# A long convolution's second stage on four frequencies at once, one in each quarter of the TensorE array

## The chip, the cores and the metric

One core of one Trainium2 chip. The time is that of the device for the whole kernel, in microseconds (us), over several runs; smaller is better.

## The reference

A long convolution by FFT along the sequence for 8 batches, then a soft mixture of experts. Cut to what matters:

```python
# x: (8, 5696, 128), h: (5696, 128), all float32
Xf = np.fft.rfft(x, n=2 * S, axis=1); Hf = np.fft.rfft(h, n=2 * S, axis=0)
x = np.fft.irfft(Xf * Hf[None], n=2 * S, axis=1)[:, :S, :].reshape(B * S, D)
logits = x @ phi                       # phi: (128, 32)
# dispatch: softmax of the logits over the tokens; experts on 32 slots;
# combine: softmax over the slots, out = c @ slot_out
```

## The kernel before

The transform is split into 90 x 64. **Stage one** (`stage_a`) multiplies blocks of x by a table of 90 frequencies and stores the result. **Stage two** (`stage_b1`, `stage_b2`) works on 45 pairs of frequencies per batch, two pairs in a *unit*, 23 units per batch: forward transform of length 64, product with the filter's transform (`Hr`, `Hi`), backward transform. **Stage three** (`stage_c1` to `stage_c6`) transforms back, computes the logits and both softmaxes. A loop of 92 steps interleaves them; one batch takes 8 steps. Stage one runs in steps 0 to 71, stage two from step 9, stage three from step 26. A step has three slots for stage-two units.

Cut to what the change and the argument touch (`...` marks cuts):

```python
ps = mid.enter_context(tc.tile_pool(name="ps", bufs=6, space=PSUM))    # bank(): a ring of 6 banks
aps = mid.enter_context(tc.tile_pool(name="aps", bufs=2, space=PSUM))
wt = fconst.tile([P, NP, P], F32, name="wt")    # P = 128, NP = 45: block-diagonal 2 x (64 x 64)
vt = fconst.tile([P, NP, P], F32, name="vt")
...
    def stage_b1(u):
        g, i = divmod(u, NU)
        n = min(2, NP - 2 * i)
        t_ = gs.pop(u)
        p = bank()
        pv = p[:, :].rearrange("p (q c d) -> p q c d", c=2, d=D)
        for q in range(n):
            nc.tensor.matmul(p[:, q * 256:(q + 1) * 256], wt[:, 2 * i + q, :],
                             t_[:, q, :, :].rearrange("p c d -> p (c d)"), start=True, stop=True)
        if g == 0:
            for q in range(n):
                m = 2 * i + q
                pr = bpool.tile([P, 2, D], F32, name="pr", tag="pr")
                for c in range(2):
                    nc.scalar.activation(pr[:, c, :], pv[:, q, c, :], AF.Copy,
                                         scale=turn[:, 0, m:m + 1])
                nc.vector.scalar_tensor_tensor(
                    out=Hr[:, m, :], in0=pv[:, q, 1, :], scalar=turn[:, 1, m:m + 1],
                    in1=pr[:, 0, :], op0=AL.mult, op1=AL.add)
                nc.vector.scalar_tensor_tensor(
                    out=Hi[:, m, :], in0=pv[:, q, 0, :], scalar=turn[:, 1, m:m + 1],
                    in1=pr[:, 1, :], op0=AL.mult, op1=AL.subtract, reverse1=True)
            return
        pr, pi = [bpool.tile([P, 2, 2, D], F32, name=f"p{c}", tag=f"p{c}") for c in "ri"]
        for t, H in ((pr, Hr), (pi, Hi)):
            nc.vector.tensor_tensor(
                out=t[:, 0:n, :, :], in0=pv[:, 0:n, :, :],
                in1=H[:, 2 * i:2 * i + n, :].unsqueeze(2).broadcast_to([P, n, 2, D]), op=AL.mult)
        y_ = bpool.tile([P, 2, 2, D], F32, name="yf", tag="yf")
        nc.vector.tensor_tensor(out=y_[:, 0:n, 0, :], in0=pr[:, 0:n, 0, :], in1=pi[:, 0:n, 1, :],
                                op=AL.subtract)
        nc.vector.tensor_tensor(out=y_[:, 0:n, 1, :], in0=pr[:, 0:n, 1, :], in1=pi[:, 0:n, 0, :],
                                op=AL.add)
        prods[u] = y_

    def stage_b2(u):
        g, i = divmod(u, NU)
        if g == 0:
            return
        n = min(2, NP - 2 * i)
        y_ = prods.pop(u)
        p = bank()
        for q in range(n):
            nc.tensor.matmul(p[:, q * 256:(q + 1) * 256], vt[:, 2 * i + q, :],
                             y_[:, q, :, :].rearrange("p c d -> p (c d)"), start=True, stop=True)
        st = bpool.tile([P, 2, 2 * D], F32, name="zst", tag="zst", bufs=3)
        nc.scalar.activation(st[:, 0:n, :], p[:, 0:n * 256].rearrange("p (q c) -> p q c", q=n),
                             AF.Copy)
        nc.sync.dma_start(
            out=zd[g - 1][2 * i:2 * i + n, :, :, :].rearrange("q r c d -> r q (c d)"),
            in_=st[:, 0:n, :])
...
    def stage_c3(T):
        ...                                       # TensorE: logits; ScalarE: lt
            nc.vector.reduce_max(out=mx[r, :], in_=lt[r, :, :, 0:MH - v], axis=AX.XYZ)   # mx
        ...
        def slot_b():
            if us:
                u = us.pop(0)
                prefetch(u + AHEAD)
                stage_b1(u)
                wait_b2.append(u)
                if len(wait_b2) > 1:
                    stage_b2(wait_b2.pop(0))
            elif wait_b2:
                stage_b2(wait_b2.pop(0))
        ...
        if t < NA:
            stage_a(t, 1)
            fold(t + 1, 1)                        # GpSimd: x of the next block
        if pair(1) is not None:
            stage_c3(pair(1))
        slot_b()
```

In the traces TensorE's matmuls and VectorE's instructions stand in the order in which they are issued here. So the backward half of a unit comes one slot after its forward half.

Of the kernel before, what the change touches and what calls it, by code (L numbers as in the profile page):

```python
# [17 lines left out]
def transform_tables(S, N1, N2, CH, Z0, X0, F0):  # L18
# [18 lines left out]
    s1 = np.pad(s1, [(X0, P - R1 - X0), (0, 0), (F0, P - N1 - F0)])  # L37
# [7 lines left out]
    NP = N1 // 2  # L45
    back = np.arange(N2).reshape(2, HALF // CH, CH).transpose(1, 0, 2).reshape(-1)
    wbd = np.zeros((2 * N2, NP, 2 * N2))
    vbd = np.zeros((2 * N2, NP, 2 * N2))
    for par in range(2):
        r = slice(par * N2, (par + 1) * N2)  # L50
        wbd[par::2, :, r] = w[par * NP:(par + 1) * NP].transpose(1, 0, 2)
        vbd[r, :, r] = w[par * NP:(par + 1) * NP][:, back].transpose(2, 0, 1)
    turn = (N1 - 1) / 2 * alpha[:, None] + (N2 - 1) / 2 * omega
    tn = np.zeros((2 * N2, 2, NP))
    for par in range(2):
        r = slice(par * N2, (par + 1) * N2)
        tn[r, 0] = np.cos(turn[par * NP:(par + 1) * NP]).T / N
        tn[r, 1] = np.sin(turn[par * NP:(par + 1) * NP]).T / N
    return [np.ascontiguousarray(t, dtype=np.float32) for t in (s1, i1, wbd, vbd, tn)]
# [3 lines left out]
def kernel(  # L63
# [24 lines left out]
    nc = tc.nc  # L88
# [18 lines left out]
    Z0, X0, F0 = 20, 20, 19  # L107
# [4 lines left out]
        for n, t in zip(("s1", "i1", "w", "v", "turn"), transform_tables(S, N1, N2, CH, Z0, X0, F0))]  # L112
    fd = [nc.dram_tensor(f"f_{g}", (N2, N1, 2, D), F32, kind="Internal").ap() for g in range(B + 1)]
# [16 lines left out]
    ypool = work.enter_context(tc.tile_pool(name="ypool", bufs=1))  # L130
    mid, inner, cload = ExitStack(), ExitStack(), ExitStack()
    ps = mid.enter_context(tc.tile_pool(name="ps", bufs=6, space=PSUM))
    aps = mid.enter_context(tc.tile_pool(name="aps", bufs=2, space=PSUM))
    front = ExitStack()
# [6 lines left out]
    wt = fconst.tile([P, NP, P], F32, name="wt")  # L141
    vt = fconst.tile([P, NP, P], F32, name="vt")
    turn = fconst.tile([P, 2, NP], F32, name="turn")
    Hr = fconst.tile([P, NP, D], F32, name="Hr")
    Hi = fconst.tile([P, NP, D], F32, name="Hi")

    def bank():
        return ps.tile([P, 512], F32, name="bank", tag="bank")
# [34 lines left out]
    def stage_a(c, comp):  # L183
# [4 lines left out]
        for G in range(2):  # L188
# [6 lines left out]
        nc.sync.dma_start(out=fd[g][n0:n0 + CH, :, :, :].rearrange("n k g d -> k n (g d)"),  # L195
                          in_=st[F0:F0 + N1, :, :, :].rearrange("k n g d -> k n (g d)"))
# [4 lines left out]
    def load_g(u):  # L201
        if u >= (B + 1) * NU:
# [6 lines left out]
            in_=fd[g].rearrange("r (a p) c d -> (r a) (p c d)",  # L209
                                a=2)[:, 4 * i * D:(4 * i + 2 * n) * D])  # L210
        gs[u] = t_

    def stage_b1(u):
# [3 lines left out]
        p = bank()  # L217
        pv = p[:, :].rearrange("p (q c d) -> p q c d", c=2, d=D)
        for q in range(n):
            nc.tensor.matmul(p[:, q * 256:(q + 1) * 256], wt[:, 2 * i + q, :],  # L220
                             t_[:, q, :, :].rearrange("p c d -> p (c d)"), start=True, stop=True)
        if g == 0:
            for q in range(n):
                m = 2 * i + q
                pr = bpool.tile([P, 2, D], F32, name="pr", tag="pr")
                for c in range(2):
                    nc.scalar.activation(pr[:, c, :], pv[:, q, c, :], AF.Copy,  # L227
                                         scale=turn[:, 0, m:m + 1])
                nc.vector.scalar_tensor_tensor(  # L229
                    out=Hr[:, m, :], in0=pv[:, q, 1, :], scalar=turn[:, 1, m:m + 1],  # L230
# [6 lines left out]
        for t, H in ((pr, Hr), (pi, Hi)):  # L237
            nc.vector.tensor_tensor(  # L238
                out=t[:, 0:n, :, :], in0=pv[:, 0:n, :, :],
                in1=H[:, 2 * i:2 * i + n, :].unsqueeze(2).broadcast_to([P, n, 2, D]), op=AL.mult)  # L240
# [522 lines left out]
```

## Time and profile before

| | before |
|---|---|
| median of all its runs | 1062.6 us |
| span of the profiled run | 1066.3 us |
| steps 0 to 9 | 60.1 us |
| steps 10 to 16 (h in stage two) | 50.7 us |
| steps 17 to 25 (stages one and two) | 85.6 us |
| steps 26 to 70 (all three stages) | 591.3 us |
| from step 71 | 278.6 us |
| one cycle of 8 steps in the middle stage | 104.8 us |

In the stretch of steps 10 to 16, the busy times of the engines (columns: stretch, length, then busy us of TensorE, its weight loads, VectorE, ScalarE, GpSimd, each with a count; the clock; the DMA share; GB/s) were:

```profile
60.10:110.80 50.70, 42.95 (x136) 24.63 (x135) 23.63 (x80) 35.98 (x107) 17.16 (x14) 1.00 0.93 279
```

DMA is at 0.93 there, so it looks as if the kernel were held by its transfers while h passes stage two. The waits of ScalarE in this stretch say otherwise (who waited for whom: us in total, times, longest):

```profile
ACT pr L227 <- DVE Hi L232: 14.7, 20, 0.7
```

It is ScalarE's only wait there. Its 36.0 us of work and these 14.7 us fill the 50.7 us: ScalarE and VectorE, which hand `pr` and its buffers to each other, set the pace (e1 below has less DMA and the same length). In the middle cycle (the third stretch that the prediction below shows) TensorE is the bound. Two lines of the waits in that cycle (who waited for whom: us in total, times, longest):

```profile
DVE mx L358 <- ACT lt L352: 8.4, 4, 2.2
PEld bank L256 <- DVE yf L244: 1.1, 2, 0.5
```

VectorE idles 8.4 us per cycle in front of `mx`. TensorE hardly ever waits for VectorE (1.1 us).

### The profile page before, as it was taken

How to read it: one execution, taken by the hardware profiler on the slowest of the kernel's cores; microseconds unless marked ns; L12 is line 12 of the kernel's file. 1: busy time of each engine (PE TensorE's matmuls, PEld its weight loads, DVE VectorE, ACT ScalarE, POOL GpSimd, SP SyncE). 2: the span in 40 equal slices, each digit the busy share in tenths (PEclk: the TensorE clock that was granted, in tenths of full speed). 3: DMA queues.
4: the chain of work that ended last, by engine and by line, in shares of the span. 5: the costliest groups of instructions: out<-in, count | busy, mean ns of one | idle time of the engine just before them, and what ended most of it. 6: DMA issues, size and time to landing. Idle time of an engine off the chain costs nothing.

```text
span 1066.3 us, 17253 instructions
## 1 busy us (share of the span) xinstructions
PE 968.4 (91%) x5690; PEld 606.3 (57%) x5690; DVE 723.7 (68%) x1384; ACT 517.1 (48%) x1049; POOL 358.5 (34%) x340
## 2 busy tenths in 40 slices
PE   6688899999999999999999999999998998775983
PEld 2255566555666666666666566656665555343683
DVE  2044566677777787777777777777778888565442
ACT  3467444455555555555555555555553434343342
POOL 5523222323433343334333333343321212384000
PEclk9899999999999999999999999999999999886855
DMA  6999999988888889888988898889877777953398
GB/s 193 288 277 289 304 333 283 296 257 258 245 274 260 265 236 282 263 257 244 279 254 270 238 276 265 259 241 278 285 214 245 247 229 214 242 158 156 135 406 340
DMA packets 175111, 275.50 MB, mean 258 GB/s; under 512 B 12864, under 2 KB 115776, under 8 KB 169263
## 3 DMA queue, kind: packets, MB, share of 16 engines
q1 hardware_dynamic: 174447, 274.04, 82.8%
q8 instruction: 47, 0.77, 0.3%
q10 hardware_dynamic: 576, 0.36, 0.1%
q14 instruction: 41, 0.34, 0.1%
HBM read 145.95 MB, written 128.39 MB: 257 GB/s over the span
## 4 chain that ended last, share of the span: by engine, by line
PE 64%; DVE 21%; DMA 8%; issue 2%; ACT 2%; POOL 1%; SPq 0%; DVEq 0%; ACTq 0%; POOLq 0%
PE bank L190 18%; PE bank L220 12%; PE bank L308 11%; PE bank L256 11%; DVE yf L242 5%; DMA out_dram<-o 4%; PE bank L338 3%; DVE pr L238 3%; DMA gt<-f 3%; DVE pi L238 3%; PE bank L348 2%; DVE y L325 2%; DVE y L324 2%; PE bank L377 2%; DVE yf L244 2%
## 5 line engine op out<-in xcount | busy, mean ns | idle before, releaser
L179 POOL TENSOR_TENSOR x<-xc 128x512 f32<-128x512 f32 x144 | 187.5, 1303 | 281.9 <-PE bank L190 237.0
L190 PE MATMUL bank<-x,s 128*128 128x512 f32 x576 | 270.6, 597 | 8.1 <-POOL x L179 8.1
L259 ACT ACTIVATE zst<-bank 128x512 f32<-128x512 f32 (+1 forms) x184 | 108.2, 588 | 296.3 <-PE bank L256 280.6
L220 PE MATMUL bank<-gt,wt 128*128 128x256 f32 x810 | 220.4, 395 | 20.1 <-DMA gt<-f 19.8
L220 PEld LDWEIGHTS bank<-gt,wt 128*128 128x128 f32 x810 | 145.4, 192 | 115.1 <-issue 54.3
L256 PE MATMUL bank<-yf,vt 128*128 128x256 f32 x720 | 189.4, 385 | 17.7 <-DVE yf L244 12.5
L192 ACT ACTIVATE fst<-bank 128x512 f32<-128x512 f32 x288 | 168.5, 598 | 67.7 <-PE bank L190 53.1
L238 DVE TENSOR_TENSOR pr<-bank,Hr 128x512 f32<-128x512 f32 (+1 forms) x184 | 124.6, 677 | 97.8 <-PE bank L220 97.7
L256 PEld LDWEIGHTS bank<-yf,vt 128*128 128x128 f32 x720 | 133.5, 190 | 53.0 <-issue 13.8
L190 PEld LDWEIGHTS bank<-x,s 128*128 128x128 f32 x576 | 107.5, 192 | 94.6 <-issue 61.8
L308 PE MATMUL bank<-zc,i 128*64 128x512 f32 x480 | 120.3, 612 | 3.5 <-DMA zc<-z 3.5
L238 DVE TENSOR_TENSOR pi<-bank,Hi 128x512 f32<-128x512 f32 (+1 forms) x184 | 123.0, 668 | 0.0
L242 DVE TENSOR_TENSOR yf<-pr,pi 128x256 f32<-128x256 f32 (+1 forms) x184 | 113.5, 617 | 6.4
L338 PE MATMUL bank<-ident,y 128*128 128x128 f32 x512 | 67.2, 289 | 15.3 <-DVE y L325 15.3
L358 DVE TENSOR_REDUCE mx<-lt 64x1 f32<-64x360 f32 x64 | 33.2, 518 | 70.1 <-ACT lt L352 69.7
L244 DVE TENSOR_TENSOR yf<-pr,pi 128x256 f32<-128x256 f32 (+1 forms) x184 | 76.5, 416 | 0.0
L338 PEld LDWEIGHTS bank<-ident,y 128*128 128x128 f32 x512 | 62.2, 150 | 20.6 <-issue 16.5
L339 ACT ACTIVATE yt<-bank 128x360 f32<-128x360 f32 x128 | 56.4, 471 | 35.6 <-PE bank L338 35.6
L229 DVE SCALAR_TENSOR_TENSOR Hr<-bank,turn,pr 128x128 f32<-128x128 f32 x45 | 15.7, 348 | 75.6 <-ACT pr L227 75.6
L324 POOL TENSOR_TENSOR y<-y,op 128x512 f32<-128x512 f32 x32 | 38.4, 1200 | 80.9 <-DVE op L313 80.9
L308 PEld LDWEIGHTS bank<-zc,i 128*64 128x64 f32 x480 | 30.1, 137 | 56.3 <-issue 53.9
L413 POOL TENSOR_TENSOR L<-L,rs 128x512 f32<-128x512 f32 x32 | 33.6, 1051 | 77.8 <-DVE rs L412 64.7
(97 smaller groups left out, 922.2 us busy)
## 6 DMA issues: line engine op xcount, KB each, us to landing
f<-fst SPq DMA_DIRECT2D x144, 360.0 KB
gt<-f SPq DMA_DIRECT2D x198, 256.0 KB
z<-zst SPq DMA_DIRECT2D x176, 256.0 KB
zc<-z SPq DMA_DIRECT2D x60, 720.0 KB
xc<-in_x_dram SPq DMA_DIRECT2D x64, 320.0 KB
out_dram<-o SPq DMA_DIRECT2D x16, 1024.0 KB
out_dram<-o SPq DMA_DIRECT2D x8, 768.0 KB
c_t<-cst SPq DMA_DIRECT2D x26, 180.0 KB
```

The source lines that it names most:

```text
L179: nc.gpsimd.tensor_tensor(out=y_[:, :, :], in0=t_[:, 0, :, :], in1=t_[:, 1, ::-1, :], op=AL.subtract if comp else AL.add)
L190: nc.tensor.matmul(p[:, :], s1[:, tab[G], :], src[:, :, :].rearrange("p n d -> p (n d)"), start=True, stop=True)
L192: nc.scalar.activation(st[:, :, G, :], p[:, :].rearrange("p (n d) -> p n d", d=D), AF.Copy)
L220: nc.tensor.matmul(p[:, q * 256:(q + 1) * 256], wt[:, 2 * i + q, :], t_[:, q, :, :].rearrange("p c d -> p (c d)"), start=True, stop=True)
L238: nc.vector.tensor_tensor(out=t[:, 0:n, :, :], in0=pv[:, 0:n, :, :], in1=H[:, 2 * i:2 * i + n, :].unsqueeze(2).broadcast_to([P, n, 2, D]), ...
L242: nc.vector.tensor_tensor(out=y_[:, 0:n, 0, :], in0=pr[:, 0:n, 0, :], in1=pi[:, 0:n, 1, :], op=AL.subtract)
L244: nc.vector.tensor_tensor(out=y_[:, 0:n, 1, :], in0=pr[:, 0:n, 1, :], in1=pi[:, 0:n, 0, :], op=AL.add)
L256: nc.tensor.matmul(p[:, q * 256:(q + 1) * 256], vt[:, 2 * i + q, :], y_[:, q, :, :].rearrange("p c d -> p (c d)"), start=True, stop=True)
L259: nc.scalar.activation(st[:, 0:n, :], p[:, 0:n * 256].rearrange("p (q c) -> p q c", q=n), AF.Copy)
L308: nc.tensor.matmul(p[h_ * HP:(h_ + 1) * HP, :], i1[:, tab, :], t_[:, o, :, q, :], start=True, stop=True)
L324: eng.tensor_tensor(out=part(v, 1), in0=part(v, 0), in1=o_[:, :, :], op=AL.subtract)
L338: nc.tensor.transpose(p[:, i * P:(i + 1) * P], ys[T][:, k * CH + i, 0:D], ident[:, :])
```

## The change

Its intent: a unit's two pairs are four frequencies, each a 64x64 product. Instead of block-diagonal 128x128 tables, half of them zeros, each frequency gets a quarter of the array, and four run at once. The tables halve. The results of the two row strips go to two different PSUM banks (the prediction names the page on which this rests), so the forward and the backward result get a two-bank tile each; to make room, the general banks go from 6 + 2 to 4. The core of the diff (the tables' construction, the store of stage one in two halves and renamings are cut):

```diff
-    ps = mid.enter_context(tc.tile_pool(name="ps", bufs=6, space=PSUM))
-    aps = mid.enter_context(tc.tile_pool(name="aps", bufs=2, space=PSUM))
+    rings = [mid.enter_context(tc.tile_pool(name="ps", bufs=4, space=PSUM))]
+    bps = front.enter_context(tc.tile_pool(name="bps", bufs=1, space=PSUM))
...
-    wt = fconst.tile([P, NP, P], F32, name="wt")
-    vt = fconst.tile([P, NP, P], F32, name="vt")
+    wt = fconst.tile([P, NP, HP], F32, name="wt")
+    vt = fconst.tile([P, NU, 2, HP], F32, name="vt")
...
-        p = bank()
-        for q in range(n):
-            nc.tensor.matmul(p[:, q * 256:(q + 1) * 256], wt[:, 2 * i + q, :],
-                             t_[:, q, :, :].rearrange("p c d -> p (c d)"), start=True, stop=True)
+        bt = bps.tile([P, 2, 512], F32, name="bt", tag="bt")
+        for a in range(2):
+            r = slice(a * HP, (a + 1) * HP)
+            for q in range(n):
+                nc.tensor.matmul(bt[q * HP:(q + 1) * HP, a, 0:2 * D], wt[r, 2 * i + q, :],
+                                 t_[r, q, :, :].rearrange("p c d -> p (c d)"),
+                                 start=True, stop=True)
...
-        p = bank()
+        bz = bps.tile([P, 2, 512], F32, name="bz", tag="bz")
         for q in range(n):
-            nc.tensor.matmul(p[:, q * 256:(q + 1) * 256], vt[:, 2 * i + q, :],
-                             y_[:, q, :, :].rearrange("p c d -> p (c d)"), start=True, stop=True)
+            r = slice(q * HP, (q + 1) * HP)
+            for a in range(2):
+                nc.tensor.matmul(bz[a * HP:(a + 1) * HP, q, 0:2 * D], vt[r, i, a, :],
+                                 y_[r, a, :, :].rearrange("p c d -> p (c d)"),
+                                 start=True, stop=True)
```

The order of the work and the operations of VectorE and ScalarE stay as they are.

More of the change, by code (lines that the diff above doesn't have):

```diff
@@ L15, with transform_tables @@
 PSUM = bass.MemoryType.PSUM
-def transform_tables(S, N1, N2, CH, Z0, X0, F0):
+def transform_tables(S, N1, N2, CH, Z0, X0, F0, F1):
     N, R1, HALF, P = N1 * N2, S // N2, N2 // 2, 2 * N2
@@ L36, in transform_tables @@
     i1 = np.stack([np.cos(a0), -np.sin(a0), -np.cos(a0)], 1)
-    s1 = np.pad(s1, [(X0, P - R1 - X0), (0, 0), (F0, P - N1 - F0)])
+    NP = N1 // 2
+    part = s1
+    s1 = np.zeros((P, 3, P))
+    for a, p in enumerate((F0, F1)):
+        s1[X0:X0 + R1, :, p:p + NP] = part[:, :, a * NP:(a + 1) * NP]
     i1 = np.pad(i1[np.arange(N1).reshape(2, N1 // 2).T.reshape(-1)],
@@ L44, in transform_tables @@
     w = np.concatenate([np.cos(a2), np.sin(a2)], 1)
-    NP = N1 // 2
     back = np.arange(N2).reshape(2, HALF // CH, CH).transpose(1, 0, 2).reshape(-1)
-    wbd = np.zeros((2 * N2, NP, 2 * N2))
-    vbd = np.zeros((2 * N2, NP, 2 * N2))
-    for par in range(2):
-        r = slice(par * N2, (par + 1) * N2)
-        wbd[par::2, :, r] = w[par * NP:(par + 1) * NP].transpose(1, 0, 2)
-        vbd[r, :, r] = w[par * NP:(par + 1) * NP][:, back].transpose(2, 0, 1)
-    turn = (N1 - 1) / 2 * alpha[:, None] + (N2 - 1) / 2 * omega
-    tn = np.zeros((2 * N2, 2, NP))
-    for par in range(2):
-        r = slice(par * N2, (par + 1) * N2)
-        tn[r, 0] = np.cos(turn[par * NP:(par + 1) * NP]).T / N
-        tn[r, 1] = np.sin(turn[par * NP:(par + 1) * NP]).T / N
-    return [np.ascontiguousarray(t, dtype=np.float32) for t in (s1, i1, wbd, vbd, tn)]
+    NU = (NP + 1) // 2
+    turn = (N1 - 1) / 2 * alpha[:, None] + (N2 - 1) / 2 * omega
+    wq = np.zeros((2, N2, NP, N2))
+    vq = np.zeros((2, N2, NU, 2, N2))
+    tn = np.zeros((2, N2, 2, NU, 2))
+    for a in range(2):
+        wq[a] = w[a * NP:(a + 1) * NP].transpose(1, 0, 2)
+        for q in range(NP):
+            vq[q % 2, :, q // 2, a] = w[a * NP + q][back].T
+            tn[q % 2, :, 0, q // 2, a] = np.cos(turn[a * NP + q]) / N
+            tn[q % 2, :, 1, q // 2, a] = np.sin(turn[a * NP + q]) / N
+    wq, vq, tn = [t.reshape(P, *t.shape[2:]) for t in (wq, vq, tn)]
+    return [np.ascontiguousarray(t, dtype=np.float32) for t in (s1, i1, wq, vq, tn)]
 @with_exitstack
@@ L106 @@
     SPLIT = R1 // 16 * 16
-    Z0, X0, F0 = 20, 20, 19
+    Z0, X0, F0, F1 = 20, 20, 6, 82
     ctx.enter_context(tc.manual_schedule())
@@ L111 @@
         nc.inline_tensor(t, f"tab_{n}").ap()
-        for n, t in zip(("s1", "i1", "w", "v", "turn"), transform_tables(S, N1, N2, CH, Z0, X0, F0))]
-    fd = [nc.dram_tensor(f"f_{g}", (N2, N1, 2, D), F32, kind="Internal").ap() for g in range(B + 1)]
+        for n, t in zip(("s1", "i1", "w", "v", "turn"), transform_tables(S, N1, N2, CH, Z0, X0, F0, F1))]
+    fd = [nc.dram_tensor(f"f_{g}", (2, N2, NP, 2, D), F32, kind="Internal").ap() for g in range(B + 1)]
     zd = [nc.dram_tensor(f"z_{b}", (NP, 2 * N2, 2, D), F32, kind="Internal").ap() for b in range(B)]
@@ L130 @@
     ypool = work.enter_context(tc.tile_pool(name="ypool", bufs=1))
+    front = ExitStack()
     mid, inner, cload = ExitStack(), ExitStack(), ExitStack()
-    ps = mid.enter_context(tc.tile_pool(name="ps", bufs=6, space=PSUM))
-    aps = mid.enter_context(tc.tile_pool(name="aps", bufs=2, space=PSUM))
-    front = ExitStack()
+    rings = [mid.enter_context(tc.tile_pool(name="ps", bufs=4, space=PSUM))]
+    bps = front.enter_context(tc.tile_pool(name="bps", bufs=1, space=PSUM))
     fconst = front.enter_context(tc.tile_pool(name="fconst", bufs=1))
@@ L140 @@
     s1 = apool.tile([P, 3, P], F32, name="s1", tag="s1", bufs=1)
-    wt = fconst.tile([P, NP, P], F32, name="wt")
-    vt = fconst.tile([P, NP, P], F32, name="vt")
-    turn = fconst.tile([P, 2, NP], F32, name="turn")
-    Hr = fconst.tile([P, NP, D], F32, name="Hr")
-    Hi = fconst.tile([P, NP, D], F32, name="Hi")
+    wt = fconst.tile([P, NP, HP], F32, name="wt")
+    vt = fconst.tile([P, NU, 2, HP], F32, name="vt")
+    turn = fconst.tile([P, 2, NU, 2], F32, name="turn")
+    Hr = fconst.tile([P, NU, 2, D], F32, name="Hr")
+    Hi = fconst.tile([P, NU, 2, D], F32, name="Hi")
     def bank():
-        return ps.tile([P, 512], F32, name="bank", tag="bank")
+        rings.append(rings.pop(0))
+        return rings[-1].tile([P, 512], F32, name="bank", tag="bank")
     xs = {}
@@ L194, in stage_a @@
         n0 = comp * HALF + CH * j
-        nc.sync.dma_start(out=fd[g][n0:n0 + CH, :, :, :].rearrange("n k g d -> k n (g d)"),
-                          in_=st[F0:F0 + N1, :, :, :].rearrange("k n g d -> k n (g d)"))
+        for a, p in enumerate((F0, F1)):
+            nc.sync.dma_start(
+                out=fd[g][a, n0:n0 + CH, :, :, :].rearrange("n q c d -> q n (c d)"),
+                in_=st[p:p + NP, :, :, :].rearrange("k n c d -> k n (c d)"))
     gs, prods = {}, {}
@@ L208, in load_g @@
             out=t_[:, 0:n, :, :].rearrange("p q c d -> p (q c d)"),
-            in_=fd[g].rearrange("r (a p) c d -> (r a) (p c d)",
-                                a=2)[:, 4 * i * D:(4 * i + 2 * n) * D])
+            in_=fd[g].rearrange("a r q c d -> (a r) (q c d)")[:, 4 * i * D:(4 * i + 2 * n) * D])
         gs[u] = t_
@@ L216, in stage_b1 @@
         t_ = gs.pop(u)
-        p = bank()
-        pv = p[:, :].rearrange("p (q c d) -> p q c d", c=2, d=D)
-        for q in range(n):
-            nc.tensor.matmul(p[:, q * 256:(q + 1) * 256], wt[:, 2 * i + q, :],
-                             t_[:, q, :, :].rearrange("p c d -> p (c d)"), start=True, stop=True)
+        bt = bps.tile([P, 2, 512], F32, name="bt", tag="bt")
[5 more added lines that the diff above has]
+                                 start=True, stop=True)
+        r = slice(0, n * HP)
+        pv = bt[r, :, 0:2 * D].rearrange("p a (c d) -> p a c d", c=2)
         if g == 0:
-            for q in range(n):
-                m = 2 * i + q
+            for a in range(2):
                 pr = bpool.tile([P, 2, D], F32, name="pr", tag="pr")
                 for c in range(2):
-                    nc.scalar.activation(pr[:, c, :], pv[:, q, c, :], AF.Copy,
-                                         scale=turn[:, 0, m:m + 1])
+                    nc.scalar.activation(pr[r, c, :], pv[:, a, c, :], AF.Copy,
+                                         scale=turn[r, 0, i, a:a + 1])
                 nc.vector.scalar_tensor_tensor(
-                    out=Hr[:, m, :], in0=pv[:, q, 1, :], scalar=turn[:, 1, m:m + 1],
-                    in1=pr[:, 0, :], op0=AL.mult, op1=AL.add)
+                    out=Hr[r, i, a, :], in0=pv[:, a, 1, :], scalar=turn[r, 1, i, a:a + 1],
+                    in1=pr[r, 0, :], op0=AL.mult, op1=AL.add)
                 nc.vector.scalar_tensor_tensor(
-                    out=Hi[:, m, :], in0=pv[:, q, 0, :], scalar=turn[:, 1, m:m + 1],
-                    in1=pr[:, 1, :], op0=AL.mult, op1=AL.subtract, reverse1=True)
+                    out=Hi[r, i, a, :], in0=pv[:, a, 0, :], scalar=turn[r, 1, i, a:a + 1],
+                    in1=pr[r, 1, :], op0=AL.mult, op1=AL.subtract, reverse1=True)
             return
@@ L238, in stage_b1 @@
             nc.vector.tensor_tensor(
-                out=t[:, 0:n, :, :], in0=pv[:, 0:n, :, :],
-                in1=H[:, 2 * i:2 * i + n, :].unsqueeze(2).broadcast_to([P, n, 2, D]), op=AL.mult)
+                out=t[r, :, :, :], in0=pv,
+                in1=H[r, i, :, :].unsqueeze(2).broadcast_to([n * HP, 2, 2, D]), op=AL.mult)
         y_ = bpool.tile([P, 2, 2, D], F32, name="yf", tag="yf")
-        nc.vector.tensor_tensor(out=y_[:, 0:n, 0, :], in0=pr[:, 0:n, 0, :], in1=pi[:, 0:n, 1, :],
+        nc.vector.tensor_tensor(out=y_[r, :, 0, :], in0=pr[r, :, 0, :], in1=pi[r, :, 1, :],
                                 op=AL.subtract)
-        nc.vector.tensor_tensor(out=y_[:, 0:n, 1, :], in0=pr[:, 0:n, 1, :], in1=pi[:, 0:n, 0, :],
+        nc.vector.tensor_tensor(out=y_[r, :, 1, :], in0=pr[r, :, 1, :], in1=pi[r, :, 0, :],
                                 op=AL.add)
@@ L253, in stage_b2 @@
         y_ = prods.pop(u)
-        p = bank()
+        bz = bps.tile([P, 2, 512], F32, name="bz", tag="bz")
         for q in range(n):
-            nc.tensor.matmul(p[:, q * 256:(q + 1) * 256], vt[:, 2 * i + q, :],
-                             y_[:, q, :, :].rearrange("p c d -> p (c d)"), start=True, stop=True)
+            r = slice(q * HP, (q + 1) * HP)
+            for a in range(2):
+                nc.tensor.matmul(bz[a * HP:(a + 1) * HP, q, 0:2 * D], vt[r, i, a, :],
+                                 y_[r, a, :, :].rearrange("p c d -> p (c d)"),
+                                 start=True, stop=True)
         st = bpool.tile([P, 2, 2 * D], F32, name="zst", tag="zst", bufs=3)
-        nc.scalar.activation(st[:, 0:n, :], p[:, 0:n * 256].rearrange("p (q c) -> p q c", q=n),
-                             AF.Copy)
+        nc.scalar.activation(st[:, 0:n, :], bz[:, 0:n, 0:2 * D], AF.Copy)
         nc.sync.dma_start(
@@ L417, in dispatch @@
     def dispatch(T):
-        ap_ = aps.tile([P, 512], F32, name="ap", tag="ap")
+        ap_ = bank()
         d_ = ds.pop(T)
@@ L541, in slot_b @@
         def slot_b():
-            if us:
+            fresh = bool(us)
+            if fresh:
                 u = us.pop(0)
@@ L546, in slot_b @@
                 wait_b2.append(u)
-                if len(wait_b2) > 1:
-                    stage_b2(wait_b2.pop(0))
-            elif wait_b2:
+            if len(wait_b2) > fresh:
                 stage_b2(wait_b2.pop(0))
-        for tab, src, first in ((wt, t_w, LAG_B - 2), (vt, t_v, LAG_B + NJ - 2)):
-            p0 = 2 * PER * (t - first)
-            if 0 <= p0 < NP:
-                p1 = min(NP, p0 + 2 * PER)
-                nc.sync.dma_start(out=tab[:, p0:p1, :], in_=src[:, p0:p1, :])
+        for tab, src, first, n, k in ((wt, t_w, LAG_B - 2, NP, 2 * PER),
+                                      (vt, t_v, LAG_B + NJ - 2, NU, PER)):
+            p0 = k * (t - first)
+            if 0 <= p0 < n:
+                v = slice(p0, min(n, p0 + k))
+                nc.sync.dma_start(out=tab[:, v], in_=src[:, v])
         if pair(1 - 2 * ahead) is not None:
@@ L603 @@
             front.close()
+            rings.append(mid.enter_context(tc.tile_pool(name="ps2", bufs=4, space=PSUM)))
             last = work.enter_context(tc.tile_pool(name="last", bufs=1))
@@ L677 @@
                 out=hidT[:, g, k0:k0 + 4, :], in_=p[:, :].rearrange("p (k c) -> p k c", k=4))
-    sop = aps.tile([P, 512], F32, name="ap", tag="ap")
+    sop = bank()
     for g in range(EG):
```

## The prediction

> **What bounds the kernel now.** I read the busy table by slices first, because a mean hides the stages. The rows are engines, one digit per fortieth of the 1066.3 us span:
>
> ```profile
> PE   6688899999999999999999999999998998775983
> DVE  2044566677777787777777777777778888565442
> DMA  6999999988888889888988898889877777953398
> ```
>
> TensorE is full from the ninth slice to about the thirtieth, VectorE stays near 0.8, and the DMA engines are never far behind: they are fuller than TensorE at the start. I then asked for the busy time of each engine in stretches. The step boundaries come from the first-stage matmuls (L190), which open each of the first 72 of 92 steps. Columns are stretch, length, then busy us (instructions) of PE, weight loads, DVE, ACT, POOL, then clock, DMA share, GB/s:
>
> ```profile
> 42.00:111.00 69.00, 51.09 (x155) 29.73 (x156) 25.52 (x86) 42.27 (x123) 20.28 (x16) 0.93 0.94 285
> 111.00:196.00 85.00, 77.46 (x271) 51.09 (x270) 51.08 (x105) 36.95 (x65) 23.90 (x19) 0.98 0.94 300
> 393.50:498.30 104.80, 104.34 (x581) 64.66 (x580) 81.98 (x153) 55.48 (x108) 39.42 (x36) 1.00 0.86 261
> 801.00:903.00 102.00, 90.29 (x588) 56.38 (x586) 85.41 (x170) 42.76 (x86) 21.48 (x24) 1.00 0.74 231
> ```
>
> So there are four stages that matter. From 42 to 196 us stages one and two run and DMA is at 0.94. From 196 to 801 us all three stages run; one of its cycles of 8 steps takes 104.8 us and TensorE works 104.34 of them: this is the stage to win, 605 us or 5.77 cycles. From 801 to 903 us the first stage is gone and VectorE (0.84) and waits between engines matter. After 903 us no second stage is left, so the change can't help the last 163 us.
>
> Inside the middle stage, the chain of waits gives start, length and count:
>
> ```profile
> 500.22 1.03 PE ap L424 x32
> 501.25 1.06 PE bank L220 x4
> ...
> 504.49 0.86 PE bank L220 x4
> 505.36 0.86 PE bank L256 x4
> 506.22 1.72 PE bank L190 x4
> 507.94 0.74 PE bank L348 x8
> 508.68 1.06 PE bank L220 x4
> 509.74 0.86 PE bank L256 x4
> ```
>
> The reader sees that one fp32 matmul leaves two records. Four records of 256 columns cost 0.86 us, so 0.215 us each. L220 (forward, two frequencies block-diagonal in one 128x128 table, two such matmuls per unit) and L256 (backward) pay 0.86 us each per unit. It costs 1.06 after L424 or L348, which split the array: 0.20 us for going back to the whole array. L348 itself is eight records of 360 columns; at 0.86/1024 us a column they would take 2.42 us one after another and 0.60 four at a time, and they take 0.74, so about 0.14 to enter the split.
>
> **What the Trainium skill says.** "TensorE: Matmul & The Clock Gate", Part 3 (Packing small matmuls), says that matmuls in different row and column strips of the array run at once, started some 4 ns apart. The trace agrees for each direction alone:
>
> ```profile
> 513.98 1.94 PE L308 MATMUL bank<-zc,i 128*64 128x512 f32 x8
> 1029.63 10.93 PE L716 MATMUL op<-so,cT 32*128 32x128 f32 x139
> ```
>
> L308 uses two column halves: eight records of 512 columns in the time in which L190 does four. L716 uses four row strips at clock 0.50: 10.93/139 = 0.079 us per record, against 0.215 for 128 columns at half clock, so 2.7 at once with waits for its readers included. Both directions together, as in the change, no instruction of this trace shows. "TensorEngine Tiling (Array Packing)", Key Properties, says that changing the tiling mode drains the engine; the 0.14 and 0.20 us above are what I take for that. The same page's Gotcha 1 says that different row tiles must not be in one PSUM bank together; this is why the results get two-bank tiles of their own. The DMA page isn't needed: the trace has its rates.
>
> **The change part by part.** Per cycle there are 23 units (45 pairs of frequencies), forward and backward.
> - Removed: 90 forward and 90 backward records, 180 x 0.215 = 38.7 us of TensorE.
> - Added: twice as many records on 64x64 quarters, four quarters at once. Every unit then takes two records deep: 0.43 us forward, 0.43 backward, 23 x 0.86 = 19.8 us. Gain 18.9 us.
> - Added: mode changes. Stage one and all transposes use the whole array; L308, L424 and L348 use other splits. In two steps I count 8 changes now and 16 after (each of the 6 visits to stage two is then a mode of its own). At 0.14 to 0.20 us that is 1.4 us now, 2.8 after: 5.8 us more per cycle of four such double steps.
> - TensorE per cycle: 104.3 - 18.9 + 5.8 = 91.2 us.
> - Weight loads: twice as many of half the columns. L308's 64-column loads keep up (3.9 us for 64 of them per cycle, inside 15.5 us of matmul), so they add nothing.
> - VectorE and ScalarE: the same number of instructions of 128x512. Only the odd last unit becomes 64 partitions x 512 instead of 128 x 256: 2 x 0.27 + 2 x 0.14 = 0.8 us per cycle. VectorE 82.0 -> 82.8.
> - DMA: the same bytes and run lengths for the intermediate; its store becomes two issues per block (144 more at about 0.34 us of SyncE, which has room). The tables lose 2.95 MB in two halves, each loaded in the DMA-bound stage at 285 to 300 GB/s: 5 us each, if the stage is held by bandwidth:
>
> ```profile
> L556 SPq DMA_DIRECT2D wt<-tab_w x8: 320/1010/2612, 38.2 to 92.1; - x8
> L556 SPq DMA_DIRECT2D vt<-tab_v x8: 428/485/582, 100.5 to 161.5; - x8
> ```
>
> - PSUM: 4 general banks instead of 6 + 2, one forward and one backward tile, each single. A forward matmul must wait until VectorE has read the last one (`pi`, L238). But the backward matmul right behind it waits for `yf` anyway, which VectorE finishes some 1.0 us later. So the new wait should seldom be the last.
>
> Middle stage: TensorE needs 91.2 us. DMA, 0.865 x 104.8 = 90.6 us at today's packet times, was never sustained above some 0.94 to 0.97 while loading, so some 95 us. VectorE needs 82.8 us. Three resources this close don't overlap perfectly. I choose 97 us per cycle: 7.8 us gained, times 5.77 is 45 us. From 42 to 196 us: 10 us for the tables, and hardly more for TensorE since DMA holds it: 10 us. From 801 to 903 us: TensorE falls from 90 to about 75 us, VectorE's 85 remain; I choose 95, a gain of 7. Sum 62 us: 1062.85 - 62 = 1000.
>
> **The rivals.**
> - *DMA becomes the bound and takes most of it.* For it: 0.86 already, 0.94 in the early stage, where an L190-and-L220 mix reached 285 to 300 GB/s against 261 now. Then a cycle can't go under about 96 us (261 x 104.8 / 285). That is close to my figure; with lengthening packets 101 us, and the total is about 1025.
> - *VectorE and the single tiles become the bound.* For it: VectorE's `yf` subtraction (L242) already stands at 8.0% of the middle cycle's chain, and the 801-903 stage ran 13% longer than its busiest engine's 90.3 us. A like loss on 91.2 us gives 103 us a cycle, total about 1040. Against: VectorE itself has 22% to spare.
> - *Quarters don't overlap four-fold.* With two at once the gain of 18.9 us vanishes and the mode changes stay: 5.8 x 5.77 = 33 us slower in the middle, total about 1085. L308 and L716 speak against it.
> - *Mode changes are nearly free between splits.* Then TensorE needs 86 us, and DMA alone holds the cycle at about 94: total about 980.
>
> **Range and chances.** The first two rivals are the likely disappointments and the last the likely surprise, so 965 to 1035. Faster by over 2% means under 1041.6 us, a third of my gain: chance 0.88. Within 2%: 0.10. Slower: 0.02, the third rival.
>
> **What would show it.** Groups of L220's successor: 180 records in a middle cycle instead of 90, TensorE busy about 12 us instead of 24.4, with starts a few ns apart in fours. TensorE busy in a middle cycle falls to about 91 us of 97, with the idle part put down to `yf` or the forward matmul waiting for VectorE. DMA share there rises to about 0.93. The 42-111 stretch shortens by about 5 us and the end after the last backward unit by nothing. I am wrong if the middle cycle stays over 101 us: then a wait on VectorE (single tile) or on a transfer will stand where L220 and L256 stood in the chain. I am also wrong if the quarters come one or two at a time.

## More of the kernel before

Group 0 of stage two is the filter h itself: it only has a forward half, whose results become `Hr` and `Hi`.

The steps are cut at the first matmul of stage one in each step, read from the trace.

## The result

The changed kernel takes 1090.3 us (median of 4), against 1061.6 us of the kernel before (median of 4 runs). The ratio is 1.026 with a 95% interval of 1.022 to 1.030: **slower by 2.6%**. (A ratio is the mean time of one kernel's fast runs over that of the other's of the same rounds, so it isn't quite the ratio of the medians.) Its profiled span is 1089.0 us.

The slices of the page of the changed kernel:

```profile
PE   6667688788898889888988898888887787775894
DVE  2033357578888888888888888888888888566452
DMA  7965589999889998989899988988977876864398
```

TensorE came down from 9 to 8 in the middle, as it should. VectorE went up from 7 to 8. And from the third to the sixth slice, where DMA was full, it is at 5 to 8 now. The same stretches as before, in the changed kernel:

```profile
62.20:142.20 80.00, 53.57 (x216) 18.47 (x213) 25.59 (x84) 40.49 (x112) 17.39 (x14) 0.79 0.61 180
417.30:521.50 104.20, 92.39 (x763) 41.53 (x761) 87.39 (x153) 56.48 (x108) 39.69 (x37) 1.00 0.89 263
```

The first is steps 10 to 16: 80.0 us instead of 50.7, with DMA down from 0.93 to 0.61 and no engine near full. The second is a middle cycle: TensorE's busy time fell by 12 us to 92.4 (91.2 were predicted), but the cycle is 104.2 us long, 0.6 less than before. By stage:

| us | before | after | difference |
|---|---|---|---|
| steps 0 to 9 | 60.1 | 62.2 | +2.1 |
| steps 10 to 16 | 50.7 | 80.0 | **+29.3** |
| steps 17 to 25 | 85.6 | 80.4 | -5.2 |
| steps 26 to 70 | 591.3 | 585.3 | -6.0 |
| from step 71 | 278.6 | 281.1 | +2.5 |
| sum | 1066.3 | 1089.0 | +22.7 |

So there are two questions. Where do 29 us in the early stage come from, and where did 12 us of TensorE time per middle cycle go?

**The early stage.** The instructions in order of time, 88 to 92 us, in the changed kernel (start, length, engine, line; in brackets the idle time before and what ended it):

```profile
88.38 0.66 PE L228 MATMUL bt<-gt,wt 64*64 64x256 f32 x8 [0.95 <-PE bank L196]
...
89.16 0.62 ACT L237 ACTIVATE pr<-bt,turn 128x128 f32<-128x128 f32 x2 [0.55 <-PE bt L228]
...
89.81 0.35 DVE L239 SCALAR_TENSOR_TENSOR Hr<-bt,turn,pr 128x128 f32<-128x128 f32 x1 [1.54 <-ACT pr L237]
90.08 0.34 DVE L242 SCALAR_TENSOR_TENSOR Hi<-bt,turn,pr 128x128 f32<-128x128 f32 x1
90.52 0.62 ACT L237 ACTIVATE pr<-bt,turn 128x128 f32<-128x128 f32 x2 [0.74 <-DVE Hi L242]
91.18 0.35 DVE L239 SCALAR_TENSOR_TENSOR Hr<-bt,turn,pr 128x128 f32<-128x128 f32 x1 [0.75 <-ACT pr L237]
91.44 0.34 DVE L242 SCALAR_TENSOR_TENSOR Hi<-bt,turn,pr 128x128 f32<-128x128 f32 x1
...
91.89 0.94 PE L228 MATMUL bt<-gt,wt 64*64 64x256 f32 x8 [2.85 <-issue]
```

The reader sees one round: forward matmul, ScalarE twice, VectorE twice, ScalarE twice, VectorE twice. `Hi` ends at 91.78, and only then, at 91.89, does the next forward matmul start, from 88.38 to 91.89 in 3.51 us. There is one `bt`, and it is held all that time. Over the 23 units of h the next forward matmul starts 3.5 to 4.8 us after the last, 3.84 in the mean; 20 of the units fall into steps 10 to 16, and 20 x 3.84 = 77 of the stretch's 80 us. Everything behind in TensorE's order waits too: its clock was granted at 0.79 (1.00 before) and the stores and loads thin out. Before, a round took even longer, 4.2 to 5.9 us from the matmul to the last `Hi`, but with six banks about two units were under way at once, and one started every 2.48 us in the mean (20 x 2.48 = 50 us).

**The middle cycle.** The chain of waits in the changed kernel through a two-step period (`...` marks cuts):

```profile
504.88 1.91 PE bank L196 x4
506.79 0.79 PE bank L360 x8
...
507.60 0.49 ACT lt L364
...
508.11 0.52 DVE mx L370
...
509.55 0.60 DVE pr L248
...
510.78 1.38 DVE yf L252
512.16 0.34 DVE yf L254
...
512.64 0.66 PE bz L268 x8
513.30 1.87 PE bank L320 x8
...
527.19 1.30 DVE yf L252
528.49 0.35 DVE yf L254
...
528.88 0.66 PE bz L268 x8
529.54 1.91 PE bank L196 x4
```

No engine is busy along the whole of it; the chain goes round. Stage one and the logits on TensorE let ScalarE write `lt`; `mx` had stood waiting for that at the head of VectorE's order; behind it come the products and `yf` of a unit whose forward half had ended as `mx` began, 1.3 us before its products; the backward matmul waits for `yf`, and behind that stands the next stage-three work. At 528.88 a backward matmul waits for `yf` again, and the next round's stage one stands behind it. The waits of the cycle say the same:

```profile
PE bz L268 <- DVE yf L254: 8.4, 8, 1.1
DVE mx L370 <- ACT lt L364: 7.8, 4, 2.0
PEld bz L268 <- DVE yf L254: 5.7, 4, 1.5
```

`mx` waits about as long as before. But TensorE, whose matmuls had hardly idled for `yf` (only 1.1 us of their weight loads' waits stand above), now idles 8.4 us for it, out of 104.2 - 92.4 = 11.8 us idle in all. (The weight loads' 5.7 us lie partly in the same time and don't add.) Two `yf` in the chain take 1.38 and 1.30 us, though those with no fold beside them take 0.42 in the mean: GpSimd's fold of x lay beside both.

### The profile page after: what moved, and what is told of

It is laid out like the page before. It is cut to its first block, busy times and chain, and to the rows that moved or that the text cites. A ratio compares the mean times of both kernels' runs of the same rounds, so it can differ in the third digit from the quotient of the medians.

```text
span 1089.0 us, 20316 instructions
## 1 busy us (share of the span) xinstructions
PE 891.5 (82%) x7220; PEld 420.1 (39%) x7220; DVE 757.7 (70%) x1386; ACT 526.9 (48%) x1051; POOL 359.9 (33%) x340
## 4 chain that ended last, share of the span: by engine, by line
PE 41%; DVE 41%; DMA 8%; issue 6%; ACT 3%; POOL 1%; SPq 1%; DVEq 0%; ACTq 0%; POOLq 0%
PE bank L196 12%; PE bank L320 11%; DVE yf L252 8%; DVE pr L248 6%; DVE pi L248 6%; DVE yf L254 5%; PE bt L228 5%; PE bz L268 4%; DMA out_dram<-o 3%; DVE y L337 3%; DVE mx L370 3%; DVE y L336 2%; DVE om L326 2%; PE bank L360 2%; DVE op L325 2%
## 5 line engine op out<-in xcount | busy, mean ns | idle before, releaser
L196 PE MATMUL bank<-x,s 128*128 128x512 f32 x576 | 296.6, 644 | 9.5 <-POOL x L185 8.2
L272 ACT ACTIVATE zst<-bz 128x512 f32<-128x512 f32 (+1 forms) x184 | 108.2, 588 | 250.6 <-PE bz L268 226.8
L228 PE MATMUL bt<-gt,wt 64*64 64x256 f32 x1620 | 142.6, 415 | 72.0 <-issue 31.4
L268 PE MATMUL bz<-yf,vt 64*64 64x256 f32 x1440 | 122.3, 394 | 54.9 <-DVE yf L254 53.1
L248 DVE TENSOR_TENSOR pr<-bt,Hr 128x512 f32<-128x512 f32 (+1 forms) x184 | 126.0, 685 | 59.3 <-PE bt L228 52.3
L252 DVE TENSOR_TENSOR yf<-pr,pi 128x256 f32<-128x256 f32 (+1 forms) x184 | 125.3, 681 | 6.4
L248 DVE TENSOR_TENSOR pi<-bt,Hi 128x512 f32<-128x512 f32 (+1 forms) x184 | 124.8, 678 | 0.0
L228 PEld LDWEIGHTS bt<-gt,wt 64*64 64x64 f32 x1620 | 45.7, 135 | 193.5 <-issue 68.9
L254 DVE TENSOR_TENSOR yf<-pr,pi 128x256 f32<-128x256 f32 (+1 forms) x184 | 97.0, 527 | 0.0
L268 PEld LDWEIGHTS bz<-yf,vt 64*64 64x64 f32 x1440 | 50.2, 133 | 107.0 <-issue 52.1
L239 DVE SCALAR_TENSOR_TENSOR Hr<-bt,turn,pr 128x128 f32<-128x128 f32 (+1 forms) x46 | 16.1, 350 | 103.3 <-ACT pr L237 103.3
L336 POOL TENSOR_TENSOR y<-y,op 128x512 f32<-128x512 f32 x32 | 38.4, 1200 | 76.6 <-DVE op L325 76.6
```

What stands on the lines that cost most here:

```text
L196: nc.tensor.matmul(p[:, :], s1[:, tab[G], :], src[:, :, :].rearrange("p n d -> p (n d)"), start=True, stop=True)
L228: nc.tensor.matmul(bt[q * HP:(q + 1) * HP, a, 0:2 * D], wt[r, 2 * i + q, :], t_[r, q, :, :].rearrange("p c d -> p (c d)"), start=True, sto ...
L248: nc.vector.tensor_tensor(out=t[r, :, :, :], in0=pv, in1=H[r, i, :, :].unsqueeze(2).broadcast_to([n * HP, 2, 2, D]), op=AL.mult)
L252: nc.vector.tensor_tensor(out=y_[r, :, 0, :], in0=pr[r, :, 0, :], in1=pi[r, :, 1, :], op=AL.subtract)
L254: nc.vector.tensor_tensor(out=y_[r, :, 1, :], in0=pr[r, :, 1, :], in1=pi[r, :, 0, :], op=AL.add)
L268: nc.tensor.matmul(bz[a * HP:(a + 1) * HP, q, 0:2 * D], vt[r, i, a, :], y_[r, a, :, :].rearrange("p c d -> p (c d)"), start=True, stop=True)
```

## The experiments

Theory A: in the early stage, the single forward tile makes h's units run one after another. Theory B: in the middle stage, TensorE, ScalarE and VectorE wait for each other in a loop that the distance of one unit and the place of `mx` close. It was hidden as long as TensorE had more work than the loop is long. Rivals: DMA is full; the single PSUM tiles hold the middle stage too; the quarters don't help at all; GpSimd's fold lengthens VectorE's work.

The table at the end has the stages of all runs. Spans are of the profiled runs, times are medians.

### e1_h_alternates: two tiles for h

The backward tile is idle while h passes. h's units take the two by turns.

```diff
-        bt = bps.tile([P, 2, 512], F32, name="bt", tag="bt")
+        k = "bz" if g == 0 and u % 2 else "bt"
+        bt = bps.tile([P, 2, 512], F32, name=k, tag=k)
```

> The changed kernel, but for the filter's own units (h, group 0, which have no backward half) the forward result goes by turns into the two PSUM tiles. Theory A (the single forward tile serialises h: one unit costs the whole round of 2 ScalarE and 2 VectorE pairs, some 3.5 us, 23 x 3.5 = 80 us for steps 10 to 17 against 51 us before): that stretch comes back to 50 to 58 us, the total falls by 20 to 30 us to 1060 to 1070. Rival (h is slow because its stores are now two DMAs each, or because the clock halves): the stretch stays at about 80 us and the total at 1090. Either way one cycle of the middle stage stays at 104 us.

Measured: correct, 1060.2 us, ratio to before 0.996 (0.993 to 1.000). Steps 10 to 16:

```profile
59.80:110.60 50.80, 39.44 (x217) 14.18 (x214) 23.51 (x80) 35.89 (x108) 17.03 (x14) 1.00 0.86 258
```

50.8 us against 80.0, and the clock is back at 1.00. The stores are still two DMAs each. ScalarE's wait for the forward matmul, 18.2 us in the changed kernel's stretch, is down to 0.4. DMA is at 0.86 here and was at 0.93 in the kernel before, over the same 51 us: bandwidth wasn't the bound before either. So Theory A holds and the 29 us were the single tile; the lower clock came with it. The middle cycle is still 104.1 us. All further variants of the changed kernel have this repair.

### e2_before_pools: the PSUM layout without the quarters

The kernel before, full-array matmuls and old tables, with `rings` of 4 banks and the single tiles, of which only the first bank is used:

```diff
+        p = bps.tile([P, 2, 512], F32, name="bt", tag="bt")[:, 0, :]     # stage_b1, was bank()
+        p = bps.tile([P, 2, 512], F32, name="bz", tag="bz")[:, 0, :]     # stage_b2, was bank()
```

> The kernel before with full-array matmuls and old tables, but with the PSUM layout of the change alone: 4 general banks, one single forward tile and one single backward tile. Theory A: steps 10 to 17 take about 80 us as in the changed kernel, so the total is 1085 to 1100, because the PSUM tiles and not the quarters cost the 31 us. The middle cycle says what the single tiles cost there: 105 to 108 us if they hardly matter (my prediction's step), 112 or more if they eat the gain of the quarters. Rival: within 10 us of 1062.

Measured: correct, 1105.6 us, ratio 1.040 (1.037 to 1.043). Steps 10 to 16 and a middle cycle:

```profile
63.50:151.90 88.40, 60.20 (x136) 31.44 (x135) 24.99 (x82) 39.41 (x109) 16.58 (x14) 0.80 0.59 178
433.40:538.10 104.70, 104.25 (x581) 64.63 (x580) 81.89 (x153) 55.37 (x108) 39.38 (x36) 1.00 0.86 261
```

The early stage is slow without any quarter in it: 88.4 us. The total passed the upper end of what I had expected by 6 us. The middle cycle is 104.7, as before. With TensorE full, single tiles and fewer banks cost nothing there; this step of the prediction holds where the loop isn't the bound.

### e3_lag2: the backward half two units behind

```diff
-            if len(wait_b2) > fresh:
+            while len(wait_b2) > (2 if fresh else 0):
                 stage_b2(wait_b2.pop(0))
...
-        y_ = bpool.tile([P, 2, 2, D], F32, name="yf", tag="yf")
+        y_ = bpool.tile([P, 2, 2, D], F32, name="yf", tag="yf", bufs=3)
```

> As e1_h_alternates, and the backward half runs two units behind the forward half instead of one. Theory B (in the middle stage TensorE and VectorE wait for each other: TensorE idles 11.8 us of 104.2, nearly all of it until yf is ready): the waits of the backward matmul for yf vanish and a middle cycle falls to 96 to 100 us, the total to 1020 to 1040. Rival DMA (0.90 busy is full): the cycle stays at 103 to 105 us with DMA at 0.9. Rival single tiles: the wait moves to the forward matmul for pi or to the backward one for ScalarE's zst, cycle over 102 us.

Measured: correct, 1017.9 us, ratio 0.956 (0.950 to 0.961). A middle cycle:

```profile
379.10:476.00 96.90, 90.79 (x762) 42.78 (x760) 89.08 (x152) 55.79 (x107) 39.39 (x37) 1.00 0.95 282
```

96.9 us, with the same single tiles and 19 GB/s more through the DMA engines. The waits of the backward matmul for `yf` are no longer among those of over 2.3 us in this cycle, and VectorE's idle time before `mx` is down from 7.9 to 0.1 us. The total came out 2 us under the expected range. Theory B holds. The rivals DMA and single tiles fall for the 104 us.

### e4_dma_light: a quarter of z's bytes (wrong results on purpose)

```diff
-[:, j * w_:(j + 1) * w_])
+[:, j * w_:j * w_ + w_ // 4])           # and the tile's part alike; on top of e1_h_alternates
```

> As e1_h_alternates, with the loads of z cut to a quarter of their bytes (wrong results on purpose): 540 KB of 3,326 KB a step less, DMA share in the middle from 0.90 to about 0.75. If DMA holds the middle cycle it falls from 104 us in proportion, to 95 us or less. Theory B: it stays within 2 us of 104.

Measured: one run, 1053.4 us, wrong. A middle cycle:

```profile
384.30:488.40 104.10, 92.30 (x763) 41.46 (x761) 87.30 (x153) 56.39 (x108) 39.65 (x37) 1.00 0.72 221
```

DMA falls from 0.90 to 0.72, and the cycle doesn't move by 0.1 us. DMA wasn't what held it.

### e6_max_late: `mx` behind the next unit's products

On top of e1_h_alternates, still one unit of distance:

```diff
-            stage_c3(pair(1))
+            maxes = stage_c3(pair(1))       # TensorE and ScalarE part; returns the VectorE part
         slot_b()
+        if pair(1) is not None:
+            maxes()
```

> As e1_h_alternates (backward half one unit behind), but VectorE's row maximum of stage three (mx) is put behind the next unit's products instead of ahead of them. VectorE idles 7.8 us of a 104.1 us cycle there until ScalarE has written lt, and the backward matmul then waits for the unit queued behind it. If the loop TensorE -> lt -> mx -> products -> yf -> backward matmul holds the cycle, breaking it at mx gives 97 to 101 us a cycle and a total of 1025 to 1045; if only the distance of one unit matters, the cycle stays over 102 us and the total near 1055.

Measured: correct, 1005.6 us, ratio 0.948 (0.945 to 0.950). Four middle cycles, cut at step starts, are 96.9, 96.9, 97.8 and 96.9 us. The total is 20 us below the range, since the part from step 71 gains too (281.1 to 266.2 us), which I hadn't reckoned with. The waits of the backward matmul in one of these cycles, of 97.8 us:

```profile
PEld bz L269 <- DVE yf L255: 5.7, 4, 1.5
PE bz L269 <- DVE yf L255: 3.9, 4, 1.0
```

The matmuls' idle time for `yf` is down from 8.4 to 3.9 us, while in e3 it is gone; VectorE's wait for `lt` in front of `mx` is gone. The loop can be opened at either place, and either way gives 97 us.

### e5_pool_light: GpSimd's fold cut to a quarter (wrong results on purpose)

```diff
-        nc.gpsimd.tensor_tensor(out=y_[:, :, :], in0=t_[:, 0, :, :], in1=t_[:, 1, ::-1, :],
+        nc.gpsimd.tensor_tensor(out=y_[:, 0:1, :], in0=t_[:, 0, 0:1, :], in1=t_[:, 1, 3:4, :],
```

> e1_h_alternates with GpSimd's fold of x cut from 512 columns to 128 (wrong results on purpose). Rival cause of the 104 us cycle: GpSimd's fold lies beside VectorE's yf, which then takes some 1.3 us instead of 0.41; VectorE's busy time rose by 5.4 us a cycle. If this is what lengthens the loop, VectorE falls to about 80 us busy and the cycle to 98 us or less. If the order of waits alone holds the cycle, it stays over 102 us.

Measured: one run, 1017.9 us, wrong. The groups of `yf` in a middle cycle, first of e1_h_alternates, then of this run:

```profile
L253 DVE TENSOR_TENSOR yf<-pr,pi 128x256 f32<-128x256 f32 (+1 forms) x23 | 18.3, 796 | 0.8
L255 DVE TENSOR_TENSOR yf<-pr,pi 128x256 f32<-128x256 f32 (+1 forms) x23 | 12.8, 556 | 0.0
```

```profile
L255 DVE TENSOR_TENSOR yf<-pr,pi 128x256 f32<-128x256 f32 (+1 forms) x23 | 11.8, 513 | 0.8
L257 DVE TENSOR_TENSOR yf<-pr,pi 128x256 f32<-128x256 f32 (+1 forms) x23 | 10.3, 449 | 0.0
```

`yf` falls from 31.1 to 22.1 us a cycle, VectorE from 87.3 to 77.7, and the cycle from 104.1 to 96.2. This rival isn't false. The fold beside `yf` is one of the links that made the loop 104 us long. It doesn't take the place of Theory B, for e3 and e6 reach the same cycle with the fold whole and VectorE at 85 to 89 us busy. How much of the 7.9 us is `yf` and how much GpSimd's own 13 us less, this run doesn't separate; in the changed kernel TensorE's weight loads waited 1.5 us a cycle for the fold.

"SBUF — State Buffer", Who interferes with whom, in the Trainium skill says that a VectorE instruction with two SBUF inputs contends with a GpSimd instruction that reads SBUF; the page's "Summary: rules for kernel authors" says that the second one to issue blocks until the first is through. The trace of the changed kernel agrees, in the instructions in order of time:

```profile
510.61 1.27 POOL L185 TENSOR_TENSOR x<-xc 128x512 f32<-128x512 f32 x1 [2.40 <-PE bank L196]
...
510.78 1.38 DVE L252 TENSOR_TENSOR yf<-pr,pi 128x256 f32<-128x256 f32 x1
```

The fold ends at 511.88, and the `yf` that had started in it ends at 512.16, 0.28 us later, 1.38 us long in place of 0.41. In the middle cycle 11 of the 46 `yf` instructions start inside a fold, and each ends 0.28 to 0.29 us after that fold; in the kernel before it is 7 of 46, with the same 0.28 to 0.29.

### e8_before_lag2 and e11_before_lag2_max_late: the repairs without the quarters

The kernel before with the distance of e3 (in e8), and with `mx` late too (in e11). For the third `yf` buffer, `pi` gives up its second one.

> The kernel before, with full-array matmuls and its own PSUM rings, and only the backward half two units behind (a third yf buffer; the second buffer of pi given up for its space). TensorE is 99.5 percent busy in its middle cycle, so if the gain of e3 comes from the quarters the cycle stays at 104 to 105 us and the total within 8 us of 1063. Rival (the distance alone made e3 fast, the quarters do nothing): cycle about 97 us, total about 1020.

> e8_before_lag2 with mx put late: the kernel before with both repairs of the order of work but full-array matmuls, to be set beside e7_lag2_max_late. TensorE is full in its middle cycle, so it should stay at 103 to 104 us there and at 1035 to 1045 in total; then the quarters are worth some 40 to 45 us in a schedule that can use them. Rival (the two repairs did it all): about 1000.

Measured: e8 correct, 1043.6 us, ratio 0.983 (0.981 to 0.986); e11 correct, 1041.3 us, ratio 0.980 (0.978 to 0.982). A middle cycle of e8:

```profile
491.20:594.80 103.60, 103.60 (x581) 64.93 (x580) 81.73 (x153) 55.39 (x108) 39.61 (x37) 1.00 0.88 264
```

TensorE is busy for every bit of it, so a change of order finds no idle time of TensorE to take away. Still e8 is 18 us faster than before in the same rounds, more than the 8 I allowed (1.7%; by the 2% line of this study e8 counts as the same and e11 as unclear). The two profiled runs are 28 us apart; 17 of these come from step 71 on, where stage one has run out and TensorE isn't full (278.6 to 261.7 us), and 7 from steps 17 to 25. The repair of the order is worth something without the quarters, but in another place.

### e7_lag2_max_late and e7b_lag2_max_late: the quarters with both repairs

> e3_lag2 with mx put late as well. If the loop was the only cause and e3 broke it, this adds nothing: 96 to 97 us a cycle, total 1012 to 1022. If VectorE's order still costs something, down to 94 and a total near 1005.

> The same kernel as e7_lag2_max_late once more, on the same chip as e11, for a direct comparison: 993 to 1003 us.

Measured: correct, 996.7 us, ratio 0.940 (0.935 to 0.945), and again beside e11 994.5 us, ratio 0.935 (0.933 to 0.937). The first run fell under both totals, the lower by 8 us; the second is in its range. The middle cycles are 93.5 to 94.8 us and one of 100.3 in the first run, 93.9 to 97.6 in the second; in one of the first run, of 94.8 us, TensorE works 91.5 and VectorE 88.0, with DMA at 0.95.

This beats both kernels. Beside e11 on the same chip the quarters are worth 1041.3 - 994.5 = 46.8 us (0.9354/0.9799 = 0.955; e11 has one buffer less for `pi`, but TensorE is as full in its middle cycle as in e8's). In the schedule of the kernel before, with h repaired, they are worth about 3 us (e1: 1060.2 against 1063.3 of before in the same rounds, 0.3%), and with the single tile for h the change costs 29.

### e9_lag2_dma_light: what holds the repaired kernel (wrong results on purpose)

e3_lag2 with e4's cut of z.

> e3_lag2 with the loads of z cut to a quarter (wrong results on purpose). In e3 DMA is at 0.95, TensorE at 0.94 and VectorE at 0.92 of a 96.9 us cycle. If DMA is what now holds it, the cycle falls to 93 to 95 us; if TensorE and VectorE do, it stays at 96 to 97.

Measured: one run, 1005.7 us, wrong; all four middle cycles 95.8 us, against 96.1 to 97.5 in e3. This lies between the two expectations: DMA costs about 1 us a cycle there, and the rest is held by TensorE (91 us of work) and VectorE (89) with the waits between them. Over the whole of steps 26 to 70 the two profiled runs differ by 12 us, 7 of them in the first cycle, which takes 96.8 us here and 104.2 in e3.

### The stages of all runs

| us | 0 to 9 | 10 to 16 | 17 to 25 | 26 to 70 | from 71 | middle cycle (mean of 4) |
|---|---|---|---|---|---|---|
| before | 60.1 | 50.7 | 85.6 | 591.3 | 278.6 | 104.8 |
| after | 62.2 | 80.0 | 80.4 | 585.3 | 281.1 | 104.1 |
| e1_h_alternates | 59.8 | 50.8 | 79.8 | 588.2 | 281.1 | 104.1 |
| e2_before_pools | 63.5 | 88.4 | 84.1 | 591.4 | 275.0 | 104.8 |
| e3_lag2 | 58.1 | 50.9 | 79.3 | 552.3 | 275.1 | 96.8 |
| e4_dma_light (wrong) | 59.2 | 50.9 | 79.7 | 584.9 | 276.8 | 104.1 |
| e5_pool_light (wrong) | 57.9 | 51.0 | 81.8 | 544.0 | 281.5 | 96.2 |
| e6_max_late | 58.4 | 52.8 | 76.6 | 550.2 | 266.2 | 97.1 |
| e7_lag2_max_late | 58.2 | 50.9 | 75.8 | 541.5 | 267.8 | 95.8 |
| e7b_lag2_max_late | 59.4 | 50.9 | 75.8 | 540.6 | 264.3 | 95.7 |
| e8_before_lag2 | 58.5 | 50.1 | 78.2 | 589.5 | 261.7 | 103.6 |
| e9_lag2_dma_light (wrong) | 59.8 | 51.7 | 78.4 | 540.5 | 273.1 | 95.8 |
| e11_before_lag2_max_late | 57.7 | 54.4 | 73.9 | 587.2 | 265.3 | 103.6 |

## Why the prediction was wrong

I predicted 1000 us (965 to 1035) and faster with a chance of 0.88. It is 1090.3 us and slower.

- **TensorE's sum was right.** 91.2 us per middle cycle were computed, 92.4 measured. Four quarters do run at once: the eight records of a unit's half take 0.66 us, entry into the split included, where four full-array records took 0.86. If all the rest is put down to the mode changes, they cost a little more than I took: 104.3 - 18.9 = 85.4, so 7.0 us in place of 5.8 (and 5.8 was a slip: four times 1.4 is 5.6).
- **The step that failed first is the PSUM one**: "the new wait should seldom be the last". It was argued from `yf` alone, so for units that have a backward half. h's units have none, and their tile is held through four turns of ScalarE and VectorE. I saw those instructions (L227 to L232) in the trace and didn't ask how many units of them had been under way at once. In place of 10 us gained before 196 us, steps 10 to 16 lost 29.3 (e1 and e2 show it).
- **The 10 us for the tables** rested on "if the stage is held by bandwidth". Steps 10 to 16 weren't: ScalarE's work and its waits for `Hi` filled them, and with h repaired (e1) they take 50.8 us as before with less DMA, so the forward table's 5 us didn't come. Steps 17 to 25 are 5.2 us shorter, but e8, with the whole tables, is 7.4 us shorter there, so this isn't shown to be the backward table's.
- **The step that failed second is** "Three resources this close don't overlap perfectly. I choose 97 us per cycle". That treats engines as pipes side by side. In the order as written they are links of one loop, and its length, not any engine's load, was 104 us. TensorE's work shrank by 12 us, and 11.8 us of idle time took its place, 8.4 of them waiting for `yf`. Either repair of the order gives 97 (e3: 96.8, e6: 97.1), so the number was right for a schedule that the change didn't have. That is luck: it was chosen from three loads side by side, and both repairs together give 95.7.
- **VectorE**: 82.8 us predicted, 87.4 measured. The same instructions took longer because more `yf` started inside a fold of GpSimd (11 in place of 7): its two operations went from 16.0 + 9.4 us to 18.3 + 12.8 a cycle.
- **The rivals**: DMA as the bound is refuted (e4). "VectorE and the single tiles" was half right. VectorE stands in the chain, but the single tiles don't hold the middle stage (e2, e3). I gave "VectorE itself has 22% to spare" as evidence against it. Here VectorE was on the critical path with 16% to spare (87.4 of 104.2 us). The sign that the prediction named for being wrong came true: the cycle stayed over 101 us, with a wait for `yf` where the backward matmul stands.
- **From 801 us**: 7 us of gain were predicted; from step 71 on it lost 2.5. The order of the work binds there too: a late `mx` gains 15 us in that stretch (e6 against e1), and the distance of two units 17 without the quarters (e8 against before), though only 6 with them (e3 against e1).

Open is how the 104 us divide among the links of the loop: taking `mx`'s wait, the distance of one unit or the fold away each gives 96 to 97, and the parts don't add.

## What to carry to other kernels

Before an engine that is full is relieved, follow the chain once around without it: write down who waits for whom in program order, and how long that round takes if the full engine took no time; that round, not the next busiest engine, can be the new bound, as it was here. When a buffer goes from a ring to a single one, look at every group of instructions that uses it, also the short one at the start, and multiply its hold time by its count. And when a saving vanishes, try the order of the work first: a move of one reduction turned 1060 us into 1006 here.

## What the Trainium skill lacked or had wrong

- "TensorEngine Tiling (Array Packing)", Key Properties, says that a change of the tiling mode drains the engine, with no time for it. Estimates from the traces here: about 0.14 us into the split of L348 and 0.20 us back to the whole array (the prediction's working), 0.66 - 2 x 0.215 = 0.23 us into the quarters; 7.0 us a middle cycle for some 32 more changes are about 0.22 us each.
- "TensorE: Matmul & The Clock Gate", Part 3, has measured speedups for four row strips, three column strips, and 3x3 and 4x4 tiles of 32x32; none for four 64x64 quarters, and it doesn't say whether they hold for fp32, where a matmul leaves two records here. Here eight records of 64x64 with 256 columns took 0.66 us, against 8 x 0.215 = 1.72 one after another.
